# An attention and mixer kernel on one core: the values' products in eight tiles of 64 rows by 32 columns, their sums in two PSUM banks

## The chip, the core and the metric

The kernel runs on one core of a Trainium2 chip. TensorE (PE in the profile, its weight loads PEld) multiplies matrices out of SBUF into PSUM, which has eight banks of 128 partitions by 512 fp32 numbers; VectorE (DVE), ScalarE (ACT) and GpSimd (POOL) do the rest; SyncE (SP) issues transfers. The metric is the device time of one execution in microseconds (us), lower is better. All numbers are fp32; "fp32r" is a form of fp32 whose matmuls the code uses in hi and lo parts.

## The reference

```python
def reference(A_x, A_wqkv, A_wo, B_x, B_w1, B_b1, B_w2, B_b2, gate_w):   # S=2048 tokens, D=640, H=32 heads of 20
    x = A_x
    g = _sigmoid((x * gate_w).sum(-1, keepdims=True))
    a = _A_ref(x, A_wqkv, A_wo)      # softmax(q k^T / sqrt(20)) v for each head, then @ wo
    b = _B_ref(x, B_w1, B_b1, B_w2, B_b2)   # layernorm, then an MLP of width 1728 across the tokens
    return g * a + (1 - g) * b
```

The change touches only the attention: for each head, o[q] = sum over the 2048 keys k of p[q, k] v[k], with p the exponentials of the scores, and the sum of the p that divides it.

## The kernel before

It has four stages in time: queries, keys and values (to about 218 us); the MLP, between whose products the first part of the score maxima is worked off (to 727 us); the attention loop (to 1698 us); the products with wo and the output.

The attention loop runs over 16 pairs p of heads (j = 0, 1 within a pair), and for each over 32 steps `it`: two halves of the queries (qh, 1024 queries each) by 16 blocks of 128 keys (kt). A step g = 32 p + it does this on TensorE, in this order, which the program's text sets (engines with a manual schedule keep the order in which the code issues):

- `st_pair(g)`: two transposed scores (keys on partitions), of the heads j = 0 and 1 for the first 512 queries of the half, each a matmul of 62 rows, at rows 0 and 64 of the array, into the two banks of the tag "two" (L1015). ScalarE takes one exponential of both, 128 x 1024 (L1022).
- `st_one(g, 0)`: the same for head 0 and the second 512 queries, one bank, an exponential of its own (L1030).
- two steps of `s_next()`: plain scores for the maxima of a later pair (L212), two banks of the tag "s", reduced on VectorE (L218). The last 23 of the 512 steps have none.
- `st_one(g, 1)`: head 1, one bank.
- `pv_flush()`: the values' products of the step before, g-1: four matmuls (L919), one for each head j and each 512 queries c. A value block of 128 keys by 32 columns (20 values, a column of ones that gives the sum of the p, padding) is the stationary operand, p the moving one, and the product goes to 32 of the 128 partitions of one bank, tag "pv", where it adds up over the 16 steps kt.

After the last of the 16 steps `pv_evac` copies that bank to SBUF on VectorE (L892), and GpSimd's queue stores it (L900, L903). The next half's first products wait for the copy, since "pv" is one bank. So the eight banks are: two (2), one0, one1, s3, pv, s (2). The single scores take one0, one1 and s3 in turn.

VectorE's order in the loop is the reductions, with the copy between them in the place where `pv_flush` stands.

Of the kernel before, what the change touches and what calls it, by code (L numbers as in the profile page):

```python
# [7 lines left out]
F32 = mybir.dt.float32  # L8
# [5 lines left out]
P = 128  # L14
S, D, H, DH, F = 2048, 640, 32, 20, 1728
NP = H // 2
NT = S // P
# [8 lines left out]
VW = DH + 1  # L26
# [5 lines left out]
def gated_mix(ctx, tc, xT, x, wqk, wv0, wv1, wo, w1, w1t, b1, w2, b2, out):  # L32
    nc = tc.nc
# [37 lines left out]
    psum = ctx.enter_context(tc.tile_pool(name="psum", bufs=1, space=PSUM))  # L71
# [12 lines left out]
    def one_tile(shape, name):  # L84
        n = one_count[0] % 4
        one_count[0] += 1
        return psum.tile(shape, F32, tag=("s3", "pv", "one0", "one1")[n], bufs=1, name=name)
# [56 lines left out]
    def base_stack(p, full, eng=nc.sync):  # L144
        ks = k8([P, S], F32R, f"ks{p}_{full}")
        qs = [q4([P, S // 2], F32R, f"qs{p}_{full}_{i}") for i in range(2)]
        load_stack(p, ks, qs, full, eng)
        return ks, qs

    def load_m(p, qs, half, put=nc.sync.dma_start):  # L150
        src = m_d[p, half].rearrange("(g i j t) r -> i j t g r", i=2, j=2, t=8)
        for j in range(2):
            for i in range(2):
                r = 64 * j + 3 * DH + i
                dst = qs[half].bitcast(F32)[r: r + 1, :].rearrange("o (t g r) -> o t g r", g=4, r=32)
                put(dst, src[i: i + 1, j])

    s_src, st_src, v_tiles = {}, {}, {}

    def load_v(p, pieces=1, put=nc.sync.dma_start):  # L160
        v_tiles[p] = (ap if p % 2 else base).tile([P, NT, NPAIR], F32, tag="v", bufs=1, name=f"v{p}")
        c0 = NPAIR * (p % 8)
        for i in range(pieces):
            kt = slice(i * NT // pieces, (i + 1) * NT // pieces)
            put(v_tiles[p][:, kt], v_d[p // 8, kt, :, c0: c0 + NPAIR].rearrange("t p c -> p t c"))
# [268 lines left out]
    for half in range(2):  # L434
        wvh, wvl = wvs[half]
        width = HALF + 2 if half == 0 else HALF
        for t in range(NT):
            n = NT * half + t
# [11 lines left out]
            ps = one_tile([P, width], f"v{half}_{t}")  # L450
# [387 lines left out]
    def s_stack(p):  # L838
        ks = lp.tile([P, S], F32R, tag="sk", bufs=2, name=f"sk{p}")
        qs = [lp.tile([P, S // 2], F32R, tag="sq", bufs=4, name=f"sq{p}_{i}") for i in range(2)]  # L840
        load_stack(p, ks, qs, False)
        return ks, qs
# [30 lines left out]
    def last_load():  # L873
        b = LAST * S // P
        rl = ap.tile([P, 256], F32, tag="rl", bufs=1, name="rl_last")
        nc.sync.dma_start(rl[:, :b], l_d[H - LAST:].rearrange("h (a b) -> (h a) b", b=b))
        last_rl.append(rl[:, :b])
# [7 lines left out]
    def norm(h0, h1, at):  # L885
        loads, recips, stores = norm_steps(h0, h1)
        for n, f in enumerate(loads + recips + stores):
            later[at if n == 0 else at + 10 + 2 * n] = f

    def pv_evac(p, qh, pv):  # L890
        ev = ap.tile([P, 512], F32, tag="oev", bufs=2, name=f"oev{p}_{qh}")
        nc.vector.tensor_copy(ev, pv)  # L892
        stores = []
        for j in range(2):
            h = 2 * p + j
            for c in range(2):
                r = 32 * (2 * j + c) + 11 * j
                cols = slice(qh * 1024 + c * 512, qh * 1024 + (c + 1) * 512)
                put = nc.sync if (p, qh) == (NP - 1, 1) else nc.gpsimd
                put.dma_start(l_d[h: h + 1, cols], ev[r + DH: r + DH + 1, :])  # L900
                stores.append((o_d[DH * h: DH * h + DH, cols], ev[r: r + DH, :]))
        for a in stores:
            nc.gpsimd.dma_start(*a)  # L903
        if qh == 1 and p in (7, 11, 13, 15):
            h0 = {7: 0, 11: 16, 13: 24, 15: 28}[p]
            if p == NP - 1:
                last_load()
            else:
                norm(h0, 2 * p + 2, 32 * p + 38)
# [3 lines left out]
    def pv_flush():  # L913
        while pend:
            p, qh, kt, pv, pt = pend.pop(0)
            for j in range(2):
                for c in range(2):
                    r = 32 * (2 * j + c)
                    nc.tensor.matmul(pv[r: r + 32, :], v_tiles[p][:, kt, VW * j: VW * j + 32], pt[j, c],  # L919
                                     start=(kt == 0), stop=(kt == NT - 1))  # L920
            if kt == NT - 1:
                pv_evac(p, qh, pv)

# [3 lines left out]
    def load_wo(c):  # L927
        raw = ap.tile([P, D], F32, tag="wor", bufs=1, name=f"wor{c}")
        nc.gpsimd.dma_start(raw, wo[c * P:(c + 1) * P, :])
        hi_lo(woh[c], wol[c], raw, hi_eng=nc.gpsimd, lo_eng=nc.gpsimd)  # L930
# [18 lines left out]
    def y_load(t):  # L949
        if 6 <= t < 10:  # L950
            ty = q4([P, D], F32, f"oy{t}")
        else:
            n = t if t < 6 else t - 4
            if n % 3 == 0:
                shape, name = [P, 3, D], f"oy{t}"
                big_y[0] = k8(shape, F32, name) if t < 6 else lp.tile(shape, F32, tag="sk", bufs=2, name=name)
            ty = big_y[0][:, n % 3]
        tys[t] = ty
        nc.sync.dma_start(ty, y_d[t * P:(t + 1) * P, :])
# [16 lines left out]
    def e_load(q):  # L976
        o_load(q, slice(0, (NC - 1) * P), NC - 1, 256, "e", 2)

    def e_high(q, pool, eng=nc.scalar):
        o_hl[q] = o_high(q, NC - 1, 256, "e", 2, pool, eng)  # L980

    def e_low(q, eng=nc.vector):
        o_low(q, "e", o_hl[q], eng)
# [26 lines left out]
    def st_mm(g, j, c, ps):  # L1010
        p, it = divmod(g, 32)
        qh, kt = divmod(it, NT)
        ks, qs = st_src[p]
        r = slice(64 * j, 64 * j + 3 * DH + 2)
        nc.tensor.matmul(ps, ks[r, kt * P:(kt + 1) * P], qs[qh][r, c * 512:(c + 1) * 512], start=True, stop=True)  # L1015
# [7 lines left out]
        pts[g] = {(j, 0): pt[:, j] for j in range(2)}  # L1023

    def st_one(g, j):
        n = (2 * g + j) % 3
        ps = psum.tile([P, 512], F32, tag=("one0", "one1", "s3")[n], bufs=1, name=f"st{g}_1{j}")
        st_mm(g, j, 1, ps)
        pt = lp.tile([P, 512], F32, tag="pt", bufs=5, name=f"p{g}_1{j}")
        nc.scalar.activation(pt, ps, AF.Exp, scale=SCALE)  # L1030
        pts[g][j, 1] = pt
# [17 lines left out]
    def first_row(it):  # L1049
        if it in (10, 21):  # L1050
            row_half(it // 21)
        for _ in range(2 if it in (14, 18, 26) else 1):
            if row_mms:
                pair64(*row_mms.pop(0))
        if it == 19:
            row_evacs.pop(0)()

    LEFT = NP * 128 + 2 - S_AHEAD
    for p in range(NP):
        qs = st_src[p][1]  # L1060
        if 8 <= p < 8 + NC:
            load_wo(p - 8)
        for it in range(32):
            qh, kt = divmod(it, NT)
            if p + 1 < NP:
                if it == 6:
                    st_src[p + 1] = base_stack(p + 1, True)
                if it == 13:
                    load_v(p + 1)
                if it == 27:  # L1070
                    load_m(p + 1, st_src[p + 1][1], 0)
            if it == 12 and p:
                load_m(p, qs, 1)
            if it == 14 and due_stack:
                n = due_stack.pop()
                if n < NP:
                    s_src[n] = s_stack(n)
            if p == NP - 1:
                if it in (0, 16, 26, 30):
                    e_load((0, 16, 26, 30).index(it))  # L1080
                if 13 <= it < 13 + NT:
                    y_load(it - 13)
                if it in (5, 24):
                    e_high(it // 24, ap, nc.gpsimd)
                    e_low(it // 24, nc.gpsimd)
            if kt == 0:
                pv = psum.tile([P, 512], F32, tag="pv", bufs=1, name=f"pv{p}_{qh}")
            take = min(LEFT - given, 2) if p or it else 0
            g = p * 32 + it
            if g:  # L1090
                st_pair(g)
                if p == NP - 1:
                    first_row(it)
                st_one(g, 0)
            else:
                pts[0] = first_p
            for _ in range(take):
                s_next()
            if g:
                st_one(g, 1)  # L1100
            given += take
            if take and given == LEFT:
                s_finish()
            pv_flush()
            if p * 32 + it in later:
                later.pop(p * 32 + it)()
            pend.append((p, qh, kt, pv, pts.pop(p * 32 + it)))
    pv_flush()
    assert not row_mms
    row_evacs.pop(0)()  # L1110
# [104 lines left out]
```

## Time and profile before

| | us |
|---|---|
| median of the runs shown (1779.09 and 1782.85) | 1780.97 |
| the profiled execution, its own time | 1777.0 |
| its span in the trace | 1775.2 |
| TensorE busy in the span | 1765.1 (99%) |
| ScalarE | 1483.9 (84%) |
| VectorE | 1225.5 (69%) |
| GpSimd | 658.3 (37%) |

Busy times are unions of an engine's records. TensorE's and ScalarE's records overlap, since both engines are pipelined: an exponential of 512 columns is a record of 619 ns on average, and the next may start before it ends. So a busy share near one doesn't tell that an engine works at its peak; starts do. The costliest rows of the page in the attention loop, with columns: line, engine, operation, tiles and shapes, count, then busy us, mean ns of one, idle us of the engine before them and what ended it:

```profile
L919 PE MATMUL pv<-p,v 128*32 128x512 f32 x4088 | 546.2, 605 | 0.0
L1022 ACT ACTIVATE p<-st 128x1024 f32<-128x1024 f32 x511 | 533.1, 1043 | 1.6 <-PE s L212 1.1
```

"128*32" is the tile of the array that a matmul takes: rows by columns. The scores read "62*128" and "60*128": they have 62 and 60 rows and take half of the array's rows.

### The profile page before, as it was taken

What the parts mean: (1) busy time and instruction counts of PE and PEld (TensorE: products, weight loads), DVE (VectorE), ACT (ScalarE), POOL (GpSimd) and SP (SyncE); (2) the same over time, 40 slices, a digit from 0 to 9 for tenths busy, and PEclk for the clock granted to TensorE, in tenths of its full rate; (3) what the DMA queues carried; (4) which work ended last, traced back from release to release, by engine and by line L of the source; (5) the groups of instructions that cost most, each with busy time, mean ns of one, the idle gap of its engine ahead of it and who ended that gap; (6) DMA issues with size and microseconds to landing.
All of it is one profiled execution on the core that took longest, in us unless ns stands there. A gap on an engine that the chain in (4) does not pass through costs nothing.

```text
span 1775.2 us, 39545 instructions
## 1 busy us (share of the span) xinstructions
PE 1765.1 (99%) x15000; PEld 1091.8 (62%) x15000; DVE 1225.5 (69%) x2380; ACT 1483.9 (84%) x2566; POOL 658.3 (37%) x989
## 2 busy tenths in 40 slices
PE   9999999999999999999999999999999999999999
PEld 6998899999999999533333333333333333333378
DVE  5303289988899889777777676776767777767245
ACT  4344388888888886799999999999999999999930
POOL 1223577789877777211211111121322121212300
PEclk9999999999999999999999999999999999999999
DMA  8767876567675564334213234043353242301553
GB/s 294 251 196 244 275 179 173 144 176 206 177 195 146 159 179 145 94 67 111 65 41 85 50 72 92 12 112 68 52 136 72 50 94 59 76 15 45 198 132 135
DMA packets 155513, 225.20 MB, mean 127 GB/s; under 512 B 66420, under 2 KB 93444, under 8 KB 151640
## 3 DMA queue, kind: packets, MB, share of 16 engines
q1 hardware_dynamic: 136698, 191.70, 39.4%
q0 software_dynamic: 15888, 25.76, 6.1%
q10 hardware_dynamic: 2736, 5.21, 1.1%
q8 instruction: 118, 1.93, 0.5%
q14 instruction: 73, 0.60, 0.1%
HBM read 166.88 MB, written 55.36 MB: 125 GB/s over the span
## 4 chain that ended last, share of the span: by engine, by line
PE 95%; DMA 3%; DVE 1%; issue 0%; POOL 0%; ACT 0%; SPq 0%; DVEq 0%; ACTq 0%; POOLq 0%
PE pv L919 29%; PE st L1015 22%; PE s L212 12%; PE y L49 10%; PE u L49 9%; PE qk L55 6%; PE v L55 4%; PE a L1124 2%; DMA wr<-in_wqk_dram 1%; DMA xr<-in_xT_dram 1%; DMA rbe<-r_d 0%; DMA rc_d<-rl_last 0%; DMA k_d<-evh 0%; DVE oy L1130 0%; PE a L49 0%
## 5 line engine op out<-in xcount | busy, mean ns | idle before, releaser
L218 DVE TENSOR_REDUCE mx<-s 128x1 f32<-128x512 f32 x1280 | 834.8, 686 | 285.7 <-PE s L212 153.1
L1030 ACT ACTIVATE p<-st 128x512 f32<-128x512 f32 x1022 | 563.9, 619 | 0.0
L919 PE MATMUL pv<-p,v 128*32 128x512 f32 x4088 | 546.2, 605 | 0.0
L1022 ACT ACTIVATE p<-st 128x1024 f32<-128x1024 f32 x511 | 533.1, 1043 | 1.6 <-PE s L212 1.1
L1015 PEld LDWEIGHTS st<-qs_True,ks_True 62*128 62x128 f32 x2044 | 245.3, 185 | 433.9 <-ACT p L1022 425.9
L1015 PE MATMUL st<-qs_True,ks_True 62*128 62x512 f32 x2044 | 494.8, 446 | 0.1
L212 PE MATMUL s<-ks_False,qs_False 60*128 60x512 f32 x1152 | 362.3, 391 | 0.3 <-ACT ov L227 0.2
L44 POOL TENSOR_TENSOR wl<-wr,wh 128x512 fp32r<-128x512 f32 x228 | 275.6, 1220 | 63.9 <-ACT wh L41 52.0
L237 DVE CUSTOM_DVE_ANT_0 ov<-s,ov 128x512 f32<-128x512 f32 x384 | 263.9, 687 | 34.2 <-PE s L212 22.6
L212 PE MATMUL s<-sk,sq 60*128 60x512 f32 x896 | 281.6, 394 | 0.0
L227 ACT ACTIVATE ov<-s 128x512 f32<-128x512 f32 x384 | 228.6, 597 | 62.4 <-PE s L212 53.4
L49 PE MATMUL y<-gh,wh 64*128 64x320 f32 x896 | 225.0, 307 | 0.0
L49 PE MATMUL y<-gl,wh 64*128 64x320 f32 x832 | 216.8, 306 | 0.0
L49 PE MATMUL y<-gh,wl 64*128 64x320 f32 x832 | 216.5, 305 | 0.0
L900 POOL DMA_DIRECT2D l_d<-oev x124 | 60.8, 497 | 409.5 <-DVE oev L892 406.8
L212 PEld LDWEIGHTS s<-ks_False,qs_False 60*128 60x128 f32 x1152 | 210.4, 184 | 3.0 <-ACT ov L227 0.8
L49 PE MATMUL u<-hh,wh 64*128 64x320 f32 x864 | 206.9, 304 | 0.0
L49 PE MATMUL u<-hl,wh 64*128 64x320 f32 x864 | 206.7, 304 | 0.0
L919 PEld LDWEIGHTS pv<-p,v 128*32 128x32 f32 x4088 | 81.6, 108 | 187.3 <-issue 174.2
L49 PE MATMUL u<-hh,wl 64*128 64x320 f32 x800 | 194.4, 304 | 0.0
L41 ACT ACTIVATE wh<-wr 128x512 fp32r<-128x512 f32 (+3 forms) x247 | 146.9, 599 | 42.8 <-PE y L49 15.2
L212 PEld LDWEIGHTS s<-sk,sq 60*128 60x128 f32 x896 | 166.2, 186 | 15.3 <-DVE mx L218 0.4
(149 smaller groups left out, 2449.1 us busy)
## 6 DMA issues: line engine op xcount, KB each, us to landing
wr<-in_w_dram SPq DMA_DIRECT2D x192, 256.0 KB
ks_True<-k_d SPq DMA_DIRECT2D x96, 160.0 KB
qs_True<-q_d SPq DMA_DIRECT2D x192, 80.0 KB
qs_False<-q_d SPq DMA_DIRECT2D x96, 80.0 KB
v_d<-vt SPq DMA_DIRECT2D x32, 212.0 KB
sk<-k_d SPq DMA_DIRECT2D x42, 160.0 KB
sq<-q_d SPq DMA_DIRECT2D x84, 80.0 KB
v<-v_d SPq DMA_DIRECT2D x15, 424.0 KB
```

Source lines behind the costliest of these rows:

```text
L41: nc.scalar.activation(hi, src, AF.Copy)
L44: (lo_eng or nc.vector).tensor_sub(lo, src, hi.bitcast(F32))
L49: nc.tensor.matmul(ps[k], a[r], b[r], start=start, stop=stop)
L55: nc.tensor.matmul(ps, a, b, start=(i == 0 and k == 0), stop=(i == n - 1 and k == 2))
L212: nc.tensor.matmul(ps, qs[half][r, t * P:(t + 1) * P], ks[r, kc * 512:(kc + 1) * 512], start=True, stop=True)
L218: nc.vector.tensor_reduce(mx[:, slot, j, t: t + 1], ps, axis=AX.X, op=OP.max)
L227: nc.scalar.activation(over[j, kc], ps, AF.Relu)
L237: nc.vector.tensor_tensor_reduce(ov, ps, ov, 1.0, -3.0e38, OP.add, OP.max, mx[:, slot, j, t: t + 1])
L919: nc.tensor.matmul(pv[r: r + 32, :], v_tiles[p][:, kt, VW * j: VW * j + 32], pt[j, c], start=(kt == 0), stop=(kt == NT - 1))
L1015: nc.tensor.matmul(ps, ks[r, kt * P:(kt + 1) * P], qs[qh][r, c * 512:(c + 1) * 512], start=True, stop=True)
L1022: nc.scalar.activation(pt, ps, AF.Exp, scale=SCALE)
L1030: nc.scalar.activation(pt, ps, AF.Exp, scale=SCALE)
```

## The change

Each value product is cut into two, over the first 64 and the last 64 of its 128 keys. The halves go to two banks: the first to "pv", the second to "s3", so a step has eight matmuls of 64 rows by 32 columns. The eviction copies one bank and adds the other. The single scores, which used s3 as their third bank, now have one0 for j = 0 and one1 for j = 1 (with the pair's two that makes four banks of transposed scores).

```diff
     def pv_evac(p, qh, pv):
         ev = ap.tile([P, 512], F32, tag="oev", bufs=2, name=f"oev{p}_{qh}")
-        nc.vector.tensor_copy(ev, pv)
+        nc.vector.tensor_copy(ev, pv[0])
+        nc.vector.tensor_add(ev, ev, pv[1])
...
                     r = 32 * (2 * j + c)
-                    nc.tensor.matmul(pv[r: r + 32, :], v_tiles[p][:, kt, VW * j: VW * j + 32], pt[j, c],
-                                     start=(kt == 0), stop=(kt == NT - 1))
+                    for k in range(2):
+                        row = slice(64 * k, 64 * k + 64)
+                        nc.tensor.matmul(pv[k][r: r + 32, :], v_tiles[p][row, kt, VW * j: VW * j + 32], pt[j, c][row],
+                                         start=(kt == 0), stop=(kt == NT - 1))
...
     def st_one(g, j):
-        n = (2 * g + j) % 3
-        ps = psum.tile([P, 512], F32, tag=("one0", "one1", "s3")[n], bufs=1, name=f"st{g}_1{j}")
+        ps = psum.tile([P, 512], F32, tag=("one0", "one1")[j], bufs=1, name=f"st{g}_1{j}")
...
             if kt == 0:
-                pv = psum.tile([P, 512], F32, tag="pv", bufs=1, name=f"pv{p}_{qh}")
+                pv = [psum.tile([P, 512], F32, tag=tag, bufs=1, name=f"{tag}{p}_{qh}") for tag in ("pv", "s3")]
```

Behind the change the same lines stand a few numbers lower: L919 becomes L922, L1015 becomes L1018, L1022 and L1030 become L1025 and L1032.

TensorE's order in a step of the loop. The names are the tiles: st_0 the pair's scores, st_10 and st_11 the single ones of j = 0 and 1, s_... the plain scores, p_0, p_10 and p_11 the exponentials, pv the sums; a name's last number is a counter. Where a matmul waits for another engine, the brackets name its semaphore. Before:

```order
L1015 MATMUL st_0_23348<-qs_True_21916,ks_True 128x512 [waits Activation_49]
L1015 MATMUL st_0_23348<-qs_True_21916,ks_True 128x512
L1015 MATMUL st_10_23353<-qs_True_21916,ks_True 128x512
L212 MATMUL s_0_5_1_1_23357<-sk_21304,sq_0_21305 128x512 [waits DVE_49]
L212 MATMUL s_0_5_0_1_23360<-sk_21304,sq_0_21305 128x512 [waits DVE_49]
L1015 MATMUL st_11_23363<-qs_True_21916,ks_True 128x512 [waits Activation_49]
L919 MATMUL pv_1_23011<-p_0_23328,v_22110 32x512
L919 MATMUL pv_1_23011<-p_10_23332,v_22110 32x512
L919 MATMUL pv_1_23011<-p_0_23328,v_22110 32x512
```

The same place after the change (s_1_25465 is the second bank of the sums):

```order
L1018 MATMUL st_0_25922<-qs_True_25154,ks_True 128x512 [waits DMAHW7_49,DMAHW6_49,DMAHW3_49]
L1018 MATMUL st_10_25927<-qs_True_25154,ks_True 128x512 [waits Activation_49]
L212 MATMUL s_1_5_1_3_25931<-sk_22545,sq_1_22547 128x512 [waits DVE_49]
L212 MATMUL s_1_5_0_3_25934<-sk_22545,sq_1_22547 128x512 [waits DVE_49]
L1018 MATMUL st_11_25937<-qs_True_25154,ks_True 128x512 [waits Activation_49]
L922 MATMUL pv_1_25464<-p_0_25896,v_24417 32x512
L922 MATMUL s_1_25465<-p_0_25896,v_24417 32x512
L922 MATMUL pv_1_25464<-p_10_25900,v_24417 32x512
L922 MATMUL s_1_25465<-p_10_25900,v_24417 32x512
L922 MATMUL pv_1_25464<-p_0_25896,v_24417 32x512
L922 MATMUL s_1_25465<-p_0_25896,v_24417 32x512
L922 MATMUL pv_1_25464<-p_11_25910,v_24417 32x512
```

The order of the groups is the same. The value products are eight, alternating between the banks, and both single scores now wait for ScalarE. What the second one waits for differs: before, the semaphore's value is that of the first exponential of the step before, after, that of the second. The value products' own wait, which stood on the last of them (not shown), is gone, since the score ahead of them waits for the same exponential.

VectorE around an eviction, before:

```order
L218 TENSOR_REDUCE mx_0_14658<-s_0_1_0_3_14861 128x1
L892 COPY oev_0_14872<-pv_0_14408 128x512
L218 TENSOR_REDUCE mx_0_14658<-s_0_2_1_0_14891 128x1
L218 TENSOR_REDUCE mx_0_14658<-s_0_2_0_0_14894 128x1
L218 TENSOR_REDUCE mx_0_14658<-s_0_2_1_1_14914 128x1
```

And after:

```order
L218 TENSOR_REDUCE mx_0_14823<-s_0_1_0_3_15055 128x1
L892 COPY oev_0_15070<-pv_0_14535 128x512
L893 TENSOR_TENSOR oev_0_15070<-oev_0_15070,s_0_14536 128x512
L218 TENSOR_REDUCE mx_0_14823<-s_0_2_1_0_15090 128x1
L218 TENSOR_REDUCE mx_0_14823<-s_0_2_0_0_15093 128x1
```

One operation of 128 x 512 more stands ahead of the next step's reductions; it reads what the copy wrote.

## The prediction

> **What bounds the kernel now.** I read the page first, then a table by stage, then the timeline of one step of the stage that the change touches, and last the places where the array changes its tiling.
>
> Stages, cut where the lines change: loads, queries, keys and values; the MLP; the attention loop; the end. Columns: window, its length, busy us and instructions of each engine, the granted clock, DMA share, GB/s.
>
> ```profile
> 218.00:727.00 509.00, 508.65 (x6296) 506.62 (x6296) 453.65 (x1121) 414.09 (x815) 400.58 (x426) 1.00 0.61 167
> 727.00:1698.00 971.00, 970.92 (x7162) 332.53 (x7161) 660.83 (x1068) 970.10 (x1533) 184.58 (x362) 1.00 0.33 76
> 1698.00:1775.20 77.20, 71.36 (x463) 67.13 (x458) 43.28 (x70) 8.83 (x10) 3.69 (x7) 0.99 0.50 154
> ```
>
> All edits lie in the loop of 971 us. There TensorE (970.92) and ScalarE (970.10) both look full, so the question is what a step is made of. The groups of the loop's lines:
>
> ```profile
> L1022 ACT ACTIVATE p<-st x511: 1024/1038/1247, 727.3 to 1695.7; 128x1024 f32<-128x1024 f32 x171
> L919 PE MATMUL pv<-p,v x4088: 592/604/618, 730.1 to 1698.4; 128*32 128x512 f32 x195
>   DVE oev L892: 11.6, 31
> ```
>
> 511 steps begin from 727.3 to 1695.7: 968.4 / 510 = 1.90 us a step. The code issues four value products a step, the trace has eight records (4088 / 511): each fp32 product runs as two passes. The last row counts how often the products waited for VectorE's eviction of the sums: 31 times, 11.6 us. One step, from the timeline (start, length, engine, line; rows of several windows):
>
> ```profile
> 1301.00 1.04 ACT L1022 ACTIVATE p<-st 128x1024 f32<-128x1024 f32 x1
> 1301.36 0.64 PE L919 MATMUL pv<-p,v 128*32 128x512 f32 x4
> 1301.81 0.61 PE L919 MATMUL pv<-p,v 128*32 128x512 f32 x4
> 1301.92 1.10 ACT L1030 ACTIVATE p<-st 128x512 f32<-128x512 f32 x2
> 1302.36 0.73 PE L1015 MATMUL st<-qs_True,ks_True 62*128 62x512 f32 x3
> 1302.40 0.62 ACT L1030 ACTIVATE p<-st 128x512 f32<-128x512 f32 x1
> 1302.69 0.39 PE L212 MATMUL s<-sk,sq 60*128 60x512 f32 x1
> 1302.92 1.02 ACT L1022 ACTIVATE p<-st 128x1024 f32<-128x1024 f32 x1
> 1302.93 0.40 PE L1015 MATMUL st<-qs_True,ks_True 62*128 62x512 f32 x1
> 1302.93 0.40 PE L212 MATMUL s<-sk,sq 60*128 60x512 f32 x1
> 1303.26 1.06 PE L919 MATMUL pv<-p,v 128*32 128x512 f32 x8
> 1303.71 0.61 PE L919 MATMUL pv<-p,v 128*32 128x512 f32 x4
> 1304.25 0.50 PE L1015 MATMUL st<-qs_True,ks_True 62*128 62x512 f32 x2
> 1304.42 0.69 DVE L892 COPY oev<-pv 128x512 f32<-128x512 f32 x1
> 1305.16 0.16 PEld L919 LDWEIGHTS pv<-p,v 128*32 128x32 f32 x8 [0.38 <-DVE oev L892]
> ```
>
> TensorE has no hole. Two passes of four value products (1301.36, 1301.81); the paired scores 0.54 after the second pass began (1302.36; one step on 1303.71 and 1304.25); the first single score with an s product (1302.69); the second single with the other s product (1302.93); the next value products 0.33 later (1303.26). Two 64-row products of one wave start together and a wave follows the last after 0.24 where nothing changes; beside a change of tiling it takes more. ScalarE starts the pair 0.92 before the first single, that 0.48 before the second, and that 0.52 before the next pair. Back to back the last would be 0.48 too, so its floor is 0.92 + 0.48 + 0.48 = 1.88 against a step of 1.90. That is the first finding: however fast the products get, the loop can gain at most 0.02 x 510 = 10 us, 0.6%.
>
> **Part 1: eight tiles in place of four.** Before, four tiles of 128 rows by 32 columns fill the array for a pass. After, eight tiles of 64 by 32 fill it for a pass, each with half the rows. The columns that stream through are the same 512 in two passes. What changes is the number of matmuls with their loads (16 records a step in place of 8), and perhaps the change of tiling on both sides of the block. The latter is the only gain on offer: before, the rows (64 to 128) and the columns (128 to 32) change together; after, the columns alone. The trace has each alone once:
>
> ```profile
> 217.48 0.39 PE L55 MATMUL qk<-xl,wh 128*128 128x512 f32 x1
> 217.70 0.40 PE L55 MATMUL qk<-xh,wl 128*128 128x512 f32 x1
> 218.03 0.42 PE L49 MATMUL u<-hh,wtmp 64*128 64x320 f32 x2
> 1698.40 0.59 PE L919 MATMUL pv<-p,v 128*32 128x512 f32 x1
> 1698.92 0.56 PE L1124 MATMUL a<-woh,ohe 128*128 128x320 f32 x2
> ```
>
> Rows alone: 0.33 in place of 0.22. Columns alone: 0.52 after a pass that streams for about 0.43 (0.45 between the passes above, of which 0.02 is the load that lengthens a first pass to 617 from 592 ns). So a change of columns alone costs 0.09, as much as both together (0.33 - 0.24 = 0.09 before the block, 0.54 - 0.43 = 0.11 behind it). I take the price as unchanged: gain 0; the other bound is all of it gone (rival A).
>
> More tiles cost starts. Eight loads begin within 0.16 - 0.11 = 0.05 us (the row at 1305.16, with a load of 0.11), and the four starts of a pass spread 0.02 us (0.64 from the first start to the last end, 0.62 for one), so 0.007 a tile: four more tiles put the end of the block 0.03 later. Bounds: 0 (starts hidden) and 0.11, one load's length. The Trainium skill (TensorE: Matmul & The Clock Gate, Measured speedup vs the span model) has about 4 ns of issue a tile; by it the term would be 0.016. I keep the row's.
>
> **Part 2: two banks for the single scores, not three.** The sums take the third bank, s3. Before, a single score waits for the exponential three singles back, done long before. After, each waits for the one two back: the second single of step g waits for the second exponential of step g-1. In the rows: that exponential runs 1302.40 + 0.62 = 1303.02, but its successor's score started at 1302.93. So the score becomes late, and behind it on TensorE stand the value products, which begin a block of 0.99 that the next pair of scores waits for, which ScalarE waits for. TensorE is in order. What a bank wait costs, from the end of the loop where singles already wait so:
>
> ```profile
> 1694.70 0.81 ACT L1030 ACTIVATE p<-st 128x512 f32<-128x512 f32 x1
> 1695.56 0.18 PEld L1015 LDWEIGHTS st<-qs_True,ks_True 62*128 62x128 f32 x1
> ```
>
> The exponential ends at 1695.51, the load starts 0.05 later: the load waits too. An unloaded product takes 0.50 where a preloaded one takes 0.40 (rows 1304.25 and 1302.93), so 0.10 more until data flow. The chain from the end of one second exponential to the end of that two steps on:
>
> - release to load 0.05, load 0.10, the wave and the change of tiling 0.33: 0.48 until the value products load (now 0.24: 1303.02 to 1303.26);
> - their block 0.99 (1303.26 to 1304.25), plus 0.03 of part 1;
> - the pair 0.50, then 0.06 until its exponential starts (1302.36 + 0.50 to 1302.92);
> - on ScalarE 0.92, 0.48 and 0.62 until that step's second exponential ends.
>
> 0.48 + 1.02 + 0.56 + 2.02 = 4.08 us for two steps: 2.04 a step, not 1.90. TensorE's own sum with the exposed load is 1.90 + 0.10 + 0.03 = 2.03, just below. ScalarE (1.88) is not full any more. Cost: 0.14 x 510 = 71 us.
>
> **Part 3: the eviction.** VectorE copies one bank and adds the other. The rows that price it (operation with a PSUM input; an operation that reads what the one before wrote; its idle time):
>
> ```profile
> L340 DVE TENSOR_TENSOR kf<-kf,qk 128x512 f32<-128x512 f32 x6 | 4.1, 677 | 0.0
> L700 DVE SCALAR_TENSOR_TENSOR ty<-y,omg,ty 128x320 f32<-128x320 f32 x1 | 0.6, 551 | 0.1
> ```
>
> So 0.68 + 0.1 more, 31 times with a restart behind it. Before, the block ends at 1303.26 + 1.06 = 1304.32, the copy ends at 1305.11 and the products load at 1305.16: the copy already ends last. After, the second bank is free at 1304.42 + 0.69 + 0.1 + 0.68 = 1305.89, products at 1305.94, 1.62 after the block. The longer step covers 0.84 + 0.14 = 0.98 of it. Left: 0.64 x 31 = 20 us. Bounds: 0 if the step's waits absorb it, 0.78 x 31 = 24; a gain is excluded, since work is only added. VectorE itself has room: in the loop it is busy 660.83 of 971 us, and the two reductions that queue behind the eviction end before their banks are asked for again. The stores of the sums follow the add on GpSimd's queue; only the last ones are on the path, as the last rows end at the tail: 0.8 us.
>
> **Sum.** 71 + 20 + 1 = 92 us on the profiled execution's 1777.0 (span 1775.2 and 1.8 around it; the median of the runs shown is 1781, 0.2% above): 1869 us, 5.2% slower.
>
> **The rivals.**
> A. The drains go. If 64 rows by 128 columns and 64 by 32 need no pause between them, the block loses 0.09 + 0.11 and the loads 0.02 + 0.10, 0.32 in all; two steps take 3.76, 1.88 a step, ScalarE's floor. Then the loop gains 0.02 x 510 = 10 us, the restarts lose up to (1.62 - 0.84) x 31 = 24, the tail 1: about 1792, no measurable change. Against it stands the row at 1698.92, where columns alone changed. The Trainium skill (TensorEngine Tiling (Array Packing), Key Properties) says that a change of mode drains the engine and lists the two shapes as different modes; by it A can't happen, and no run shows 64 by 32 yet.
> B. The row halves don't run side by side. Then a block streams four passes, 0.86 more, TensorE's sum is 2.89 a step, and the time 1777 + 0.99 x 510 + 1 = 2283. Against it: the rows at 1302.93, two 64-row tiles at once into two banks.
> C. The bank wait costs nothing, because the steps shift and ScalarE runs ahead. Then only the starts and part 3 remain: 0.03 x 510 + 24 + 1, about 1817; less if the starts hide too, 1802. Against it: the chain above is closed, each link by program order or by a bank.
> D. The load of the waiting score runs ahead of its matmul, which alone waits. Then its 0.10 goes, two steps take 3.98, and the time is 1869 - 0.05 x 510 = 1843. Against it: the row at 1695.56, a load that starts behind the release, where loads with nothing to wait for start a wave early. The Trainium skill (TensorE: Matmul & The Clock Gate, Part 2: What happens when you issue a matmul) says that the engine's queue pulls weight loads ahead of matmuls in flight; the trace agrees where nothing waits and differs where something does, and the measurement decides.
> E. The products get faster, with half the rows streaming at twice the rate. Nothing in the trace shows it, and ScalarE's floor leaves 10 us, which the restarts take back: about 1792.
>
> **Chances and range.** The forecast 0.70, with an own range of 1840 (starts hidden -8, two thirds of the restarts -13, 0.01 less latency in each step, -5) to 1900 (a load's length for the starts, +20, and 0.02 more latency in each step, +10). A 0.08, B 0.05, C 0.06, D 0.08, E 0.01, and 0.02 that ScalarE's floor is wrong. The range 1790 to 1900 takes in A, C, D and E and leaves out B and the forecast's tails. A measurement of this kernel tells about 2% (36 us) from no change. Slower: the forecast, B, D and half of C, 0.86, taken as 0.85; within 2%: A, E, the other half of C and some of the forecast's lower tail, 0.13; faster: 0.02.
>
> **What would show it.** Right: steps of 2.04 us; the load of the second single score (L1018 after the change) 0.05 behind an exponential of L1032 and named as waiting for it; ScalarE idle before the pair's exponential; the value products of a pass starting as eight; 0.09 to 0.11 still lost on both sides of the block; 31 waits of the products for the add, above 1 us from block to block. Wrong: steps of 1.88 to 1.90 with scores still loaded ahead (A or C), 1.99 with the load ahead of the release (D), or passes that start in fours 0.43 apart, four of them a step (B).

## The result and the profile after

The changed kernel takes 1860.59 us (1859.57 to 1861.62, two runs) against 1780.97: a ratio of 1.0456, 95% interval 1.0435 to 1.0477. It is slower by 4.6%; the forecast was 1869 us, 5.2% on the profiled execution. Its span is 1857.8 us.

By stage, the attention loop and the end behind it (columns as before). The two stages ahead of them are what they were, 218 and 509 us:

```profile
727.00:1780.00 1053.00, 1052.60 (x11258) 431.67 (x11258) 681.96 (x1099) 1003.80 (x1533) 183.98 (x362) 1.00 0.31 70
1780.00:1857.80 77.80, 71.59 (x458) 68.54 (x456) 44.00 (x71) 8.83 (x10) 3.68 (x7) 0.98 0.50 152
```

The loop is 82 us longer, the end 0.6. TensorE still has a record in every microsecond of the loop (1052.60 of 1053.00), but ScalarE now has room: 1003.80 of 1053, where it had been 970.10 of 971. The pair's exponentials say the same (minimum, median, maximum in ns, first and last start, and who kept the engine idle before them):

```profile
L1025 ACT ACTIVATE p<-st x511: 1024/1025/1028, 727.0 to 1777.2; 128x1024 f32<-128x1024 f32 x171
  PE st L1018: 24.1, 33
```

Before, they went up to 1247 ns with a median of 1038; now all are near the shortest. I read a longer record as an exponential that queues behind another, which no run shows by itself. The idle row (24.1 us, 33 times) is that of the 31 restarts and two more places: in run 5 below, where the restarts are not stretched, it reads 2.0 us, 2 times. The step is (1777.2 - 727.0) / 510 = 2.06 us, with the 31 stretched steps in it; those take 2.72 each, the others 2.01 on average. The timeline of two steps (start, length, engine, line):

```profile
1301.37 0.60 ACT L1032 ACTIVATE p<-st 128x512 f32<-128x512 f32 x1
1302.02 0.18 PEld L1018 LDWEIGHTS st<-qs_True,ks_True 62*128 62x128 f32 x1
1302.08 1.02 ACT L1025 ACTIVATE p<-st 128x1024 f32<-128x1024 f32 x1
1302.11 0.42 PE L1018 MATMUL st<-qs_True,ks_True 62*128 62x512 f32 x1
1302.45 0.61 PE L922 MATMUL pv<-p,v 64*32 64x512 f32 x1
1302.50 0.61 PE L922 MATMUL s<-p,v 64*32 64x512 f32 x1
1302.91 0.59 PE L922 MATMUL pv<-p,v 64*32 64x512 f32 x1
1303.47 0.50 PE L1018 MATMUL st<-qs_True,ks_True 62*128 62x512 f32 x2
1303.47 0.60 ACT L1032 ACTIVATE p<-st 128x512 f32<-128x512 f32 x1
1303.81 0.61 PE L212 MATMUL s<-sk,sq 60*128 60x512 f32 x2
1304.01 1.03 ACT L1025 ACTIVATE p<-st 128x1024 f32<-128x1024 f32 x1
1304.13 0.18 PEld L1018 LDWEIGHTS st<-qs_True,ks_True 62*128 62x128 f32 x1
1304.13 0.50 PE L1018 MATMUL st<-qs_True,ks_True 62*128 62x512 f32 x1
1304.56 0.61 PE L922 MATMUL pv<-p,v 64*32 64x512 f32 x1
1306.12 1.02 ACT L1025 ACTIVATE p<-st 128x1024 f32<-128x1024 f32 x1
```

The steps alternate: 1.93 (1302.08 to 1304.01) and 2.11 (1304.01 to 1306.12), 4.04 for the two, and so they do throughout the loop (medians 1.92 and 2.12). In the long one the wait is in plain sight. The second exponential of the step before ends at 1303.47 + 0.60 = 1304.07; the load of this step's second single score starts at 1304.13, and its matmul takes 0.50, so it waited for its weights. Both scores' neighbours on TensorE had been done on time: the s products ran from 1303.81. The value products follow at 1304.56, 0.43 after that load. In the short step the load stands at 1302.02, again 0.05 behind an exponential's end (1301.37 + 0.60; the 0.06 above is rounding), but so early that most of it is covered. The eight value products of a pass start together (1302.45 to 1302.50), the second pass 0.46 later, and the pair 0.56 after that.

Before the change, the load of the second single score ran ahead of the end of that exponential (1302.40 + 0.62 = 1303.02, shown in the prediction):

```profile
1302.70 0.19 PEld L1015 LDWEIGHTS st<-qs_True,ks_True 62*128 62x128 f32 x1
```

The starts of the traces say it for the whole loop. In the 478 steps g = 3 to 480, the load before the change starts 0.29 to 0.34 ahead of that end. After the change it never does: it starts 0.05 behind it in 449 of the 478 steps, and in the other 29, each the one behind a restart, about 0.5 behind it.

Who released the loads of the scores, before and after (idle us of the load queue, times). Before:

```profile
  ACT p L1022: 425.9, 508
  ACT p L1030: 1.7, 2
```

After:

```profile
  ACT p L1032: 225.9, 330
  ACT p L1025: 213.7, 255
```

The rows are not 226 us of loss, and not a count of the bank waits. 510 of these waits, before and after, are of the pair's load, 0.84 us each, since the load queue idles behind every block anyway; after, 255 of them are put down to each line. The other 75 of L1032's 330 are of the second single's load, 0.16 each; in the other steps its wait is too short to be listed here.

The eviction, at one of the 31 restarts (timeline):

```profile
1023.41 0.69 DVE L892 COPY oev<-pv 128x512 f32<-128x512 f32 x1
1024.20 0.69 DVE L893 TENSOR_TENSOR oev<-oev,s 128x512 f32<-128x512 f32 x1
1024.35 0.14 PEld L922 LDWEIGHTS pv<-p,v 64*32 64x32 f32 x2 [0.24 <-DVE oev L892]
1024.94 0.10 PEld L922 LDWEIGHTS s<-p,v 64*32 64x32 f32 x1 [0.47 <-DVE oev L893]
```

The add starts 0.10 after the copy's end and ends at 1024.89. One product is loaded at 1024.35, into the bank that the copy has freed; the next, into the other bank, stands 0.59 behind it, and six more stand behind that one. The products alternate between the banks, so only one of the four for the freed bank gets ahead of the add; no run issued those four first.

### The profile page after: what moved, and what is told of

Its sections match the earlier page's. It is cut to its first block, busy times and chain, and to the rows that moved or that the text cites. A ratio compares the mean times of both kernels' runs of the same rounds, so it can differ in the third digit from the quotient of the medians.

```text
span 1857.8 us, 47293 instructions
## 1 busy us (share of the span) xinstructions
PE 1848.4 (99%) x19096; PEld 1194.1 (64%) x19096; DVE 1247.7 (67%) x2412; ACT 1517.4 (82%) x2566; POOL 656.6 (35%) x989
## 4 chain that ended last, share of the span: by engine, by line
PE 97%; DMA 1%; DVE 1%; issue 0%; POOL 0%; SPq 0%; ACT 0%; DVEq 0%; ACTq 0%; POOLq 0%
PE pv L922 27%; PE st L1018 22%; PE s L212 13%; PE y L49 10%; PE u L49 9%; PE qk L55 7%; PE v L55 4%; PE s L922 2%; PE a L1126 2%; DMA rbe<-r_d 1%; DMA rc_d<-rl_last 0%; DVE oy L1132 0%; DMA wr<-in_wqk_dram 0%; PE a L49 0%; DVE mx L218 0%
## 5 line engine op out<-in xcount | busy, mean ns | idle before, releaser
L922 PE MATMUL pv<-p,v 64*32 64x512 f32 x4088 | 571.6, 601 | 0.0
L1025 ACT ACTIVATE p<-st 128x1024 f32<-128x1024 f32 x511 | 523.6, 1025 | 49.5 <-PE st L1018 24.1
L1018 PEld LDWEIGHTS st<-qs_True,ks_True 62*128 62x128 f32 x2044 | 261.8, 183 | 467.4 <-ACT p L1032 225.9
L922 PE MATMUL s<-p,v 64*32 64x512 f32 x4088 | 553.7, 601 | 0.0
L1032 ACT ACTIVATE p<-st 128x512 f32<-128x512 f32 x1022 | 552.7, 598 | 0.1
L1018 PE MATMUL st<-qs_True,ks_True 62*128 62x512 f32 x2044 | 548.0, 459 | 0.5 <-DVE ty L699 0.5
L922 PEld LDWEIGHTS pv<-p,v 64*32 64x32 f32 x4088 | 93.3, 104 | 129.0 <-issue 120.6
```

Of the source, the lines that this page charges most:

```text
L922: nc.tensor.matmul(pv[k][r: r + 32, :], v_tiles[p][row, kt, VW * j: VW * j + 32], pt[j, c][row], start=(kt == 0), stop=(kt == NT - 1))
```

## The experiments

The theory: the time is made by the third bank that the single scores lose (a bank wait ahead of the block of value products), and by the longer eviction at the restarts. The rival: the tiles make it, that is, sixteen passes with their loads and the changes of tiling. Every ratio below is to the kernel before, run on the same chip with it.

**1. The bank alone.** The kernel before, with the singles' line of the change:

```diff
-        n = (2 * g + j) % 3
-        ps = psum.tile([P, 512], F32, tag=("one0", "one1", "s3")[n], bufs=1, name=f"st{g}_1{j}")
+        ps = psum.tile([P, 512], F32, tag=("one0", "one1")[j], bufs=1, name=f"st{g}_1{j}")
```

> The kernel before with one edit: the single scores have two banks in place of three (the sums stay in one bank, four tiles). Theory of the bank wait: the second single waits for the second exponential of the step before; steps alternate between two lengths, 2.01 us on average, 0.11 more than before; no stall at the restarts, since the copy alone fits the longer step; 1777 + 0.11 x 510 = 1833 us (1820 to 1845). Rival, the eight tiles and their loads and starts make the time: the third bank was not needed, steps of 1.90, 1775 to 1785 us.

Measured: 1836.25 us against 1777.87, ratio 1.0328 (1.0313 to 1.0344). Its pair exponentials, and one of the loads in its timeline with the exponential ahead:

```profile
L1022 ACT ACTIVATE p<-st x511: 1024/1024/1043, 728.2 to 1755.1; 128x1024 f32<-128x1024 f32 x171
...
1299.86 0.60 ACT L1029 ACTIVATE p<-st 128x512 f32<-128x512 f32 x1
1300.51 0.18 PEld L1015 LDWEIGHTS st<-qs_True,ks_True 62*128 62x128 f32 x1 [0.16 <-ACT p L1029]
```

The step is (1755.1 - 728.2) / 510 = 2.01 us, as expected, and the load starts 0.05 behind the exponential's end at 1300.46; so it does in each of the steps g = 3 to 480. With not one tile changed, 58 of the 80 us are there. The rival falls as the main cause.

**2 and 3. The tiles and the eviction without the bank.** Eight banks don't hold both sums and three singles, so a bank was freed by leaving out the plain scores of head j = 0 in the loop. The control is the kernel before with that; the third run is the change with that, and the freed bank given to the singles (in both, the last 22 steps have two banks for them). The lines of the third run that matter:

```diff
     def s_one(p, half, t, mx, j, kc, slot):
         def f():
+            if half_s[0] and j == 0:
+                return
...
-        ps = psum.tile([P, 512], F32, tag=("one0", "one1")[j], bufs=1, name=f"st{g}_1{j}")
+        n = (2 * g + j) % 3 if g < 32 * NP - 22 else j
+        ps = psum.tile([P, 512], F32, tag=("one0", "one1", "sb")[n], bufs=1, name=f"st{g}_1{j}")
```

> Control for the next run: the kernel before, with the plain scores of head j = 0 left out of the attention loop (their maxima are not computed there), so that one of the plain scores' two banks is free; singles in three banks but for the last 22 steps, which have two. The wave of the second single stays, so both theories expect steps of 1.90 and the time of before, 1770 to 1785 us, 2 us more for the last steps included.

> The changed kernel with the same plain scores left out, and the bank that this frees given to the singles as their third (again but for the last 22 steps): eight tiles and the longer eviction without the bank wait. Theory of the bank wait: 0.03 a step for the starts and 31 restarts of 0.7: 14 + 22 us over the control, 1805 to 1820 us, steps that no longer alternate. Rival, the tiles make the time: as slow as the changed kernel, 75 us or more over the control.

Measured: the control 1780.64 us, ratio 1.0016 (1.0007 to 1.0025); with eight tiles 1813.40 us, ratio 1.0199 (1.0182 to 1.0216). The difference is 32.8 us, where 36 were expected. The pairs of the control:

```profile
L1028 ACT ACTIVATE p<-st x511: 1024/1145/1247, 729.6 to 1700.0; 128x1024 f32<-128x1024 f32 x171
```

And with eight tiles, the pairs' group, their starts and a load of a second single in the timeline:

```profile
L1031 ACT ACTIVATE p<-st x511: 1023/1024/1045, 726.9 to 1730.2; 128x1024 f32<-128x1024 f32 x171
...
1300.73 1.02 ACT L1031 ACTIVATE p<-st 128x1024 f32<-128x1024 f32 x1
1302.65 1.02 ACT L1031 ACTIVATE p<-st 128x1024 f32<-128x1024 f32 x1
1304.56 1.02 ACT L1031 ACTIVATE p<-st 128x1024 f32<-128x1024 f32 x1
1302.45 0.19 PEld L1024 LDWEIGHTS st<-qs_True,ks_True 62*128 62x128 f32 x1
```

The steps no longer alternate: 1.92 and 1.91, against 1.90 in the control ((1700.0 - 729.6) / 510). The load at 1302.45 is a wave ahead of its matmul, as before the change. In the two traces the steps without a restart differ by 0.015 (means of 1.916 and 1.901), 7 us in all, and the 31 with one take 2.74, 0.82 more, which is 26 us. So eight tiles gain nothing where no bank is short. The sum came out because two errors offset each other: the starts had been expected at 14 and the restarts at 22.

**4. The block in another place.** The change, with the value products of step g-2 issued between the two plain scores of step g:

```diff
-            for _ in range(take):
-                s_next()
+            if take:
+                s_next()
+            pv_flush(1)
+            if take == 2:
+                s_next()
             if g:
                 st_one(g, 1)
...
-            pv_flush()
```

> The changed kernel with the value products one step later and in another place: those of step g-2 between the two plain scores of step g, ahead of the second single, whose bank wait then lies behind the block. Banks, tiles, eviction and all counts of instructions are those of the change. Theory: the chain over the bank is cut, TensorE's sum of 0.23 + 0.33 + 1.02 + 0.34 = 1.92 us is the step, and the restarts stay (31 x 0.7): 1777 + 10 + 22 + 1 = 1810 us (1798 to 1825). Rival, tiles and drains make the time: 1850 us or more.

Measured: 1865.23 us, ratio 1.0494 (1.0476 to 1.0512). The expected number failed by 55 us, and the rival's fits. But the timeline shows the bank wait again, in another place:

```profile
1302.89 1.13 ACT L1032 ACTIVATE p<-st 128x512 f32<-128x512 f32 x2
1303.55 0.18 PEld L1018 LDWEIGHTS st<-qs_True,ks_True 62*128 62x128 f32 x1 [0.30 <-ACT p L1032]
1303.55 0.50 PE L212 MATMUL s<-sk,sq 60*128 60x512 f32 x1
1303.98 0.61 PE L922 MATMUL pv<-p,v 64*32 64x512 f32 x1
```

The load at 1303.55 is the first single's. It waits for the first exponential of the step before, the earlier of the two that begin at 1302.89 (0.61 long, to 1303.50), which is itself late, since the second single of two steps back came late behind its block. I had taken only the second single's wait into account and had not asked what the first one waits for once it stands last ahead of the block. This leaves two readings: the bank wait moved, or the order is bad by itself. The last run tests the order.

**5. The eviction alone.** The change without its add:

```diff
         nc.vector.tensor_copy(ev, pv[0])
-        nc.vector.tensor_add(ev, ev, pv[1])
```

> The changed kernel with the add left out of the eviction, so that the second half of each block of keys is missing from the attention's sums. Nothing waits for VectorE longer than before. Theory: the 31 stretched steps go, 31 x 0.7 = 22 us less than the changed kernel, which leaves the bank wait and the starts: 1.034 to 1.037 times the kernel before, 1836 to 1844 us. Rival, the stretched steps come from the restart of eight tiles and not from the add: 1855 us or more.

Measured: 1840.92 us against 1778.03, ratio 1.0348 (1.0330 to 1.0365). That is 0.0108, some 19 us, below the changed kernel's ratio. The pairs' group, and who kept ScalarE idle before it:

```profile
L1024 ACT ACTIVATE p<-st x511: 1024/1025/1035, 726.0 to 1758.4; 128x1024 f32<-128x1024 f32 x171
  PE st L1017: 2.0, 2
```

(1758.4 - 726.0) / 510 = 2.02 us a step, where the change has 2.06: 0.035 x 510 = 18 us for 31 restarts, 0.58 each. The time lies 0.2% above the first run's, which has four tiles and the same banks; the two intervals overlap, so the starts of four more tiles are worth some 4 us, which these runs tell neither from nothing nor from the 7 of the forecast.

**6. That order with three banks.** The edit of run 4 in the kernel before:

> The order of the run before (the value products of step g-2 between the plain scores) in the kernel before: four tiles, three banks for the singles. In that run the wait went over to the first single, which now stands ahead of the block and waited for the first exponential of the step before. Theory: with three banks it waits for an older one, so this order alone costs nothing: steps of 1.90, 1772 to 1790 us. Rival, the order or the products' lag itself made that run slow: 1820 us or more.

Measured: 1783.81 us, ratio 1.0030 (1.0020 to 1.0040). Who released the loads of the scores there (idle us, times):

```profile
  ACT p L1030: 16.8, 20
  ACT p L1022: 3.1, 5
```

And in run 4, with the same order and two banks:

```profile
  ACT p L1032: 119.7, 463
  ACT p L1025: 8.4, 10
```

The single exponentials (L1030 and L1032) released the loads 463 times with two banks and 20 times with three. Of the 463, 450 are of the first single's load, 0.24 us each; of the 20, none. In the steps g = 3 to 480 of run 4 that load starts 0.05 behind the end of the first exponential of the step before, but for the 29 steps behind a restart; in run 6 the median start is 0.33 ahead of that end. With four tiles the order alone costs 0.3%. So in run 4 the two banks make the wait, ahead of whichever single stands last before the block. The same order with eight tiles and three banks was not run, so that the whole of run 4's time comes of the banks and the restarts is argued, not shown.

No run beat the kernel before.

## Why the prediction was right, point by point

- **What bounds the loop.** Right: before, TensorE and ScalarE were both full at 1.90 us a step. That the change could gain at most 10 us was argued from ScalarE's starts and not tried by itself; no run came below the kernel before. In the trace before, the spacing ahead of a pair does fall to 0.48 (in some 40 of 510 steps), but single steps are as short as 1.86, so the floor of 1.88 is good to 0.02 and no better.
- **Part 1, the drains.** Right. A change of the columns alone costs what the change of both did: 0.33 from the second single's wave to the value products before, 0.34 after in the short step (1302.11 to 1302.45, with a little of the load left in it); from the second pass to the pair 0.54 before, 0.56 after. I put the 0.02 down to the longer spread of starts. Rival A is out, and by run 3 too: 1.91 a step with three banks, not 1.88. The Trainium skill (TensorEngine Tiling (Array Packing), Key Properties) says that changing the tiling mode drains the engine. The rows around 64 by 32 agree: 0.34 in place of 0.24 ahead of the block, and 0.56 behind its second pass, where one pass follows the other after 0.46.
- **Part 1, the starts.** Taken as 0.03 on the block, 7 us. The block reads 1303.47 - 1302.45 = 1.02 against 0.99: right in size. In the time it is some 4 us by runs 1 and 5 and 7 us by the steps of run 3.
- **Part 2, the bank wait.** The mechanism is right to the row: 0.05 from release to load, the load not ahead of the release, 0.43 from load to value products, two steps in one chain. The chain was 4.08 for two steps and measured 4.04 (1302.08 to 1306.12). The predicted 64 us of it without the starts measured 58 (run 1). The excess of 0.04 lies in two links, both read from a step in which ScalarE was full: from the pair's matmul to its exponential 0.54 (1303.47 to 1304.01) in place of 0.56, and the second exponential's record 0.60 in place of 0.62. The other links stand as forecast. Rival D (the load runs ahead) is out by the row at 1304.13. That the steps would alternate was not foretold, though a chain over two steps allows it. With it falls TensorE's own sum of 2.03 a step, which exposed a load in each: the load is exposed in every second step only (a record of 0.50 at 1304.13, of 0.42 at 1302.11).
- **Part 3, the eviction.** Add of 0.69 and a wait of 0.10 for the copy's result: right to 0.01. 20 us predicted, about 19 measured (run 5 against the change).
- **The tail.** 0.8 predicted; the end stage grew by 0.6.
- **Sum.** 92 us forecast; 80 measured between the medians, and 82.6 between the two spans. The terms that were too large are the chain (64 for 58) and, as far as the runs tell, the starts. The runs of before in that first comparison lay 4 us above the profiled execution on which the sum stands, so the time came 8 us from the forecast and the difference 12: that the time is the closer of the two is luck.
- **Rivals B, C and E.** B: eight products of a pass start within 0.05 us and run together. C: run 1 alone refutes it. E: a pass still takes 0.46 to the next. The forecast's own range, 1840 to 1900, held the time; the part of the range below it stood for A, C and E alone.

What stays open: how much of the starts' 0.03 reaches the end of the program (the intervals of runs 1 and 5 overlap), and whether the drain could be avoided with another tiling, which no run tried.

## What to carry to other kernels

Before you give a bank to something else, look up which older reader the next writer of each remaining bank waits for, and what stands behind that writer on its engine. Here a wait of a tenth of a microsecond ahead of a block that nothing overtook came back as a longer step, and moving the block moved the wait to the next writer. Cutting a matmul into row halves that fill the same array at the same time saved nothing by itself, and the second bank of partial sums made the eviction longer at the place where the next sums wait for it.

## What the runs showed of the hardware beside that

- The length of an exponential's record differs between kernels for the same shape: 1024 to 1247 ns before (median 1038), 1024 to 1028 after, and 1024 to 1247 with a median of 1145 in the control of run 2. The long ones are in kernels at 1.90 us a step. But run 6 has a median of 1018 (1016 to 1056) at 1.91 a step, so a short record doesn't tell that the loop is slow or ScalarE idle.
- The chain over two steps settled into a long and a short one, 2.11 and 1.93 us, although both steps have the same groups of instructions; with four tiles (run 1) too, where the medians are 2.12 and 1.90.
- The number of matmul records in the loop went from 7162 to 11258 and the loads with it, and the block grew by no more than 0.03: 16 loads of value blocks begin within 0.08 us (the first at 1302.45, the last at 1302.53):

```profile
1302.45 0.10 PEld L922 LDWEIGHTS pv<-p,v 64*32 64x32 f32 x1 [0.25 <-issue]
1302.53 0.11 PEld L922 LDWEIGHTS s<-p,v 64*32 64x32 f32 x1
```
